# A fused attention and gated feed-forward kernel: attention steps gathered behind the first product, weights loaded in another order

## Chip, core and metric

The kernel runs on one core of a Trainium2 chip. A core has five engines that work at the same time, each through its own queue in order: TensorE (PE, matrix products), VectorE (DVE), ScalarE (ACT), GpSimd (POOL) and SyncE (SP, which here issues the transfers). The metric is the device time of one execution in microseconds (us).

## The reference

```python
B, H, S, D = 8, 8, 576, 64
scores = q @ k.T / sqrt(D)                       # per batch and head
gamma  = 1 - 2.0 ** (-5 - arange(H))
Dmat   = where(i >= j, gamma ** (i - j), 0)      # causal decay
x      = ((scores * Dmat) @ v)                   # to (B*S, H*D) = (4608, 512)
h      = x @ w_in                                # 512 -> 1024
u      = h * exp(h - max(h)) / sum(exp(h - max(h)))
ln     = (u - mean(u)) / sqrt(var(u) + 1e-6) * g_ln
out    = ln @ w_out                              # 1024 -> 512, float32
```

Attention has no softmax over positions: it is linear with a decay, so it can be done in chunks with a running state (the sum of k times v, decayed).

## The kernel before

The 4608 rows are worked in 36 chunks of 128 rows. The chunks of two batches alternate: for each pair of batches there are four chunks of each (c = 0 to 3), then one chunk made of the last 64 rows of both (c = 4). So a group of nine chunks repeats four times.

A chunk n goes through these steps, each a helper in the code:

- `ld` loads q, k and v (SP), `cast` scales q and v by powers of gamma and turns all three into 16 bit (three POOL instructions; for chunks 0 and 1 q on VectorE and k on ScalarE).
- `transpose_qk` turns q16 and k16 on TensorE into `tp`; `evict_qk` copies that to `qkT` (VectorE).
- `scores` makes `sc` (TensorE, half-size weights of 64 rows), `mask` multiplies it with a triangle `tris` into `ret` (VectorE, two instructions).
- `state` makes `kp` = k times v (TensorE, weights of 64 columns); `state_update` adds it on VectorE to the old state (`t`) and makes on POOL the decayed 16-bit copy `s16` and, for c < 3, the 32-bit `s32`.
- `values` makes `x` from `ret` and v (64 columns), and from the state (full weights, for c > 0); `evict_x` copies it to `xT` (ScalarE).
- `mm1`, the first product: `xT` by w_in into `h`, 8 matmuls. `row_max` (VectorE), `exps` (ScalarE, with the sum), `solu` (VectorE: u = h times e, its sum, and nmu, minus its mean).
- `spread` (ScalarE: sum of squares of u + nmu) and `root` (three tiny POOL instructions w1, w2, rs): the factor of the row.
- `transpose_u` (TensorE), `evict_u` (ScalarE), `mm2`, the second product by w_out, 8 matmuls, and `store` (ScalarE scales by rs, SP stores).

u itself is transposed, not u minus its mean. The mean is taken out through the weights: `mean_w_out` and `centre_w_out` subtract from w_out (times g_ln) the mean over its 1024 rows.

The order on every engine is the order in which the code is written (`tc.manual_schedule()`, line 469). A start written out by hand (lines 470 to 569) treats chunks 0 and 1 together, with both first products in one call, and the loop at line 571 runs i from 3 to 34. In row i TensorE does: transposes of q and k of i+1, first product i, scores i+1, second product i-2, state and values i+1, transposes of u i-1. POOL does: the casts of i+2, `root` of i-1, s16 and s32 of i+1. An end (lines 596 to 613) treats the last chunk in halves.

PSUM tiles other than `h` come from one pool of four (`ps`): a new tile waits until the one four before it has been read. Load tiles have six buffers.

The transfers stand on SP in this order: the small table, chunk 0, chunk 1, w_in in four pieces, w_out in four, chunks 2 to 5. The identity and the triangles are constants loaded on ScalarE's queue.

Of the kernel before, what the change touches and what calls it, by code (L numbers as in the profile page):

```python
# [12 lines left out]
P = 128  # L13
H = 8
D = 64
LAG = 2


def _np_tables():


    g = 1.0 - 2.0 ** (-5.0 - np.arange(H, dtype=np.float64))
    p = np.arange(P)
    gq = (g[None, :] ** p[:, None]) / 8.0
    gk = g[None, :] ** (-p[:, None])
    gqt = (g[None, :] ** (p % 64)[:, None]) / 8.0
    gkt = g[None, :] ** (-(p % 64)[:, None])


    gs = np.zeros((P, 4))  # L30
    gd = np.zeros((P, 4, 2))
    for e in range(2):
        for hp in range(4):
            gs[e * 64 : e * 64 + 64, hp] = g[2 * hp + e] ** 128.0
        gd[e * 64 : e * 64 + 64, :, e] = gs[e * 64 : e * 64 + 64]
    small = np.concatenate([gq, gk, gqt, gkt, gs, gd.reshape(P, 8)], axis=1).astype(np.float32)
    tri = (p[None, :] >= p[:, None]).astype(np.float32)
    trit = tri * ((p[None, :] // 64) == (p[:, None] // 64))
    tris = np.concatenate([tri, trit], axis=1).astype(np.float32)
    return small, tris, np.eye(P).astype(np.float16)  # L40
# [3 lines left out]
def kernel(  # L44
# [19 lines left out]
    small_np, tris_np, id_np = _np_tables()  # L64

    const = ctx.enter_context(tc.tile_pool(name="const", bufs=1))
    load = ctx.enter_context(tc.tile_pool(name="load", bufs=6))
    half = ctx.enter_context(tc.tile_pool(name="half", bufs=4))
# [3 lines left out]
    utp = ctx.enter_context(tc.tile_pool(name="utp", bufs=LAG + 1))  # L72
# [13 lines left out]

# [4 lines left out]

# [10 lines left out]
    w_in16 = const.tile([P, 4, DFF], F16, name="w_in16")  # L102
    w_out16 = const.tile([P, NF, DM], F16, name="w_out16")
    gq, gk = small[:, 0:8], small[:, 8:16]
# [4 lines left out]
    T = {}  # L109

# [12 lines left out]
    def cast(n, first=False):  # L123
        qf, kf, vf = T.pop(("ld", n))
        tail = chunks[n][1] == 4
        a, b = (gqt, gkt) if tail else (gq, gk)
        q16 = half.tile([P, H, D], F16, name="q16")
        k16 = half.tile([P, H, D], F16, name="k16")
        v16 = half.tile([P, H, D], F16, name="v16")
        eq = nc.vector if first else nc.gpsimd  # L130
        eq.tensor_tensor(  # L131
            out=q16, in0=qf, in1=a.unsqueeze(2).to_broadcast([P, H, D]), op=ALU.mult
        )
        if first:
            nc.scalar.copy(out=k16, in_=kf)
        else:
            nc.gpsimd.tensor_copy(out=k16, in_=kf)  # L137
# [3 lines left out]
        T["h", n] = q16, k16, v16  # L141

# [42 lines left out]
    def state(n):  # L185

        (b,), c = chunks[n][0], chunks[n][1]
        _, k16, v16 = T["h", n]
        kp = ps.tile([P, 4, D], FP, tag="ps", name="kp")
        for hp in range(4):  # L190
            for e in range(2):
                nc.tensor.matmul(  # L192
                    out=kp[64 * e : 64 * e + 64, hp], lhsT=k16[:, 2 * hp + e],
                    rhs=v16[:, 2 * hp + e], start=True, stop=True,
                )
        T["kp", n] = kp

    def state_update(n):
# [5 lines left out]
        else:  # L204
            nc.vector.tensor_tensor(out=t, in0=kp, in1=T["s32", b], op=ALU.add)  # L205

        s16 = stp.tile([P, 4, 2, D], F16, tag=f"s16_{b % 2}", name="s16")
# [11 lines left out]
    def values(n):  # L219
        bs, c = chunks[n]  # L220
        ret = T.pop(("ret", n))
        _, _, v16 = T.pop(("h", n))
        qkT = T.pop(("qkT", n))
        x = ps.tile([P, 4, P], FP, tag="ps", name="x")
        s16 = [T.pop(("s16", b, c)) for b in bs] if c > 0 else []
        w = P // len(bs)

        for hp in range(4):
            for e in range(2):
                nc.tensor.matmul(  # L230
                    out=x[64 * e : 64 * e + 64, hp], lhsT=v16[:, 2 * hp + e],
                    rhs=ret[e][:, hp], start=hp == 0, stop=not s16, skip_group_check=True,
                )
        for hp in range(4):
            for i, s in enumerate(s16):
                nc.tensor.matmul(  # L236
                    out=x[:, hp, i * w : (i + 1) * w], lhsT=s[:, hp].rearrange("p e d -> p (e d)"),
                    rhs=qkT[:, 0, hp, i * w : (i + 1) * w],
                    start=False, stop=i == len(s16) - 1, skip_group_check=True,
                )  # L240
        T["x", n] = x

# [6 lines left out]
    def mm1(*ns):  # L249

        xTs = [T.pop(("xT", n)) for n in ns]
        hs = [ps_h.tile([P, DFF], FP, tag="h", name="h") for n in ns]
        order = [(i, dc) for i in range(2) for dc in range(4)]
        if len(ns) > 1:
            order.sort(key=lambda o: o[1])
        for dc in range(4) if len(ns) > 1 else (None,):
            for xT, h in zip(xTs, hs):
                for i, d in order:
                    if dc in (None, d):
                        nc.tensor.matmul(  # L260
                            out=h[:, i * 512 : (i + 1) * 512], lhsT=xT[:, d],
                            rhs=w_in16[:, d, i * 512 : (i + 1) * 512],
                            start=d == 0, stop=d == 3,
                        )
        for n, h in zip(ns, hs):
            T["hps", n] = h
# [33 lines left out]
    def solu_halves(n):  # L300
        T["u", n] = []
        for h, (e, s) in zip(T.pop(("hps", n)), T["e", n]):
# [5 lines left out]
            T["u", n].append((u, su))  # L308

# [8 lines left out]

    def spread_halves(n):
        (u0, su0), (u1, su1) = T["u", n]  # L320
        (_, s0), (_, s1) = T["e", n]
        s, su, nmu = (tiny.tile([P, 1], FP, name=x) for x in ("s", "su", "nmu"))
        nc.vector.tensor_tensor(out=su, in0=su0, in1=su1, op=ALU.add)
        nc.vector.tensor_scalar(
            out=nmu, in0=su, scalar1=-1.0 / DFF, scalar2=None, op0=ALU.mult, op1=ALU.bypass
        )
        nc.gpsimd.tensor_tensor(out=s, in0=s0, in1=s1, op=ALU.add)
        sss = []
        for u in (u0, u1):
            sq = moe.tile([P, 512], F16, tag="sqh", name="sqh")  # L330
            ss = tiny.tile([P, 1], FP, tag="ssh", name="ssh")
            nc.scalar.activation(out=sq, in_=u, func=ACT.Square, bias=nmu, accum_out=ss)
            sss.append(ss)
        ss = tiny.tile([P, 1], FP, name="ss")
        nc.gpsimd.tensor_tensor(out=ss, in0=sss[0], in1=sss[1], op=ALU.add)
        root(n, s, ss)

    def row_max(n):
        nm = tiny.tile([P, 1], FP, name="nm")
        nc.vector.tensor_reduce(out=nm, in_=T["hps", n], axis=AX.X, op=ALU.max, negate=True)  # L340
        T["nm", n] = nm

    def exps(n):
        e = moe.tile([P, DFF], FP, name="e")
        s = tiny.tile([P, 1], FP, name="s")
        nc.scalar.activation(  # L346
            out=e, in_=T["hps", n], func=ACT.Exp, bias=T.pop(("nm", n)), accum_out=s
        )
        T["e", n] = e, s

    def solu(n):
        e, s = T["e", n]
        u = moe.tile([P, DFF], F16, name="u")
        su = tiny.tile([P, 1], FP, name="su")
        nmu = tiny.tile([P, 1], FP, name="nmu")
        nc.vector.scalar_tensor_tensor(  # L356
            out=u, in0=T.pop(("hps", n)), scalar=1.0, in1=e, op0=ALU.mult, op1=ALU.mult,
            accum_out=su,
        )
        nc.vector.tensor_scalar(  # L360
            out=nmu, in0=su, scalar1=-1.0 / DFF, scalar2=None, op0=ALU.mult, op1=ALU.bypass
        )
        T["u", n] = u, nmu

    def spread(n):

        u, nmu = T["u", n]
        _, s = T.pop(("e", n))
        sq = moe.tile([P, DFF], F16, name="sq")
        ss = tiny.tile([P, 1], FP, name="ss")  # L370
        nc.scalar.activation(out=sq, in_=u, func=ACT.Square, bias=nmu, accum_out=ss)  # L371
        root(n, s, ss)

    def root(n, s, ss):
        w1 = tiny.tile([P, 1], FP, name="w1")
        w2 = tiny.tile([P, 1], FP, name="w2")
        rs = tiny.tile([P, 1], FP, name="rs")
        nc.gpsimd.tensor_scalar(
            out=w1, in0=s, scalar1=s, scalar2=1e-6 * DFF, op0=ALU.mult, op1=ALU.mult
        )  # L380
        nc.gpsimd.tensor_tensor(out=w2, in0=w1, in1=ss, op=ALU.add)  # L381
        nc.gpsimd.tensor_tensor(out=rs, in0=w2, in1=mhalf, op=ALU.pow)  # L382
        T["rs", n] = rs

    def transpose_u(n):
        u, _ = T["u", n]
        lp = ps.tile([P, NF, P], F16, tag="ps", name="lp")
        for c in range(NF):
            nc.tensor.transpose(out=lp[:, c], in_=u[:, c * P : (c + 1) * P], identity=ident)  # L389
        T["lp", n] = lp  # L390

    def evict_u(n, copy=None):
        uT = utp.tile([P, NF, P], F16, name="uT")
        (copy or nc.scalar.copy)(out=uT, in_=T.pop(("lp", n)))  # L394
        T["uT", n] = uT

    def mm2(n, parts=1):

        uT = T.pop(("uT", n))
        T["o", n] = []  # L400
# [243 lines left out]
```

## Time and profile before

| | us |
|---|---|
| time, median of 3 runs | 236.75 (235.94 to 238.74) |
| span of the profiled execution, first to last instruction | 233.8 |
| first product of chunks 0 and 1 starts | 15.06 |
| first product of chunks 2, 3, 4, 5, 6, 7 starts | 32.18, 37.91, 43.50, 49.10, 55.00, 60.66 |
| first product of chunk 35 starts | 216.45 |
| first instruction on q(0), k(0), v(0) | 5.36, 6.81, 8.13 |
| ScalarE's casts of w_in's four pieces start | 12.86, 14.10, 15.64, 16.67 |
| cast of v(3) starts, after a wait for its transfer | 30.20 |

In the profile, "busy" is the time in which an engine works on an instruction. Matmuls are pipelined: a group starts when its first matmul does, and the pitch of the starts tells its cost (0.216 us for 512 columns, 0.056 for 128, at full clock). PE's clock is either full or half. Lines such as L208 are lines of the kernel below the heading above; x8 means eight instructions put together.

### The profile page before, as it was taken

The page shows a single profiled execution, that of the slowest core. Times are in us where ns is not written, and L with a number is a line of the kernel's source. Part 1 is how long each engine was busy: PE and PEld are TensorE (multiplying, and loading weights), DVE is VectorE, ACT ScalarE, POOL GpSimd, SP SyncE. Part 2 cuts the span into 40 slices and gives each one's busy share as a digit, 9 for nine tenths or more (in the row PEclk, how much of TensorE's full clock was granted, in tenths as well). Part 3 has the DMA queues.
Part 4 walks back from the last instruction along what each step waited for, and adds up shares of the span by engine and source line. Part 5 has one row for each costly group of instructions (what it writes and reads, how often), then busy time and mean ns, then how long its engine had stood idle before and what let it go on. Part 6 is the DMA issues. An engine that isn't in the chain of part 4 may idle for free.

```text
span 233.8 us, 5779 instructions
## 1 busy us (share of the span) xinstructions
PE 209.8 (90%) x2128; PEld 114.8 (49%) x2128; DVE 177.1 (76%) x304; ACT 169.4 (72%) x267; POOL 177.6 (76%) x282
## 2 busy tenths in 40 slices
PE   0584789999999999999999999999999999999770
PEld 0331454555555555555555555555555555555340
DVE  1536699888888888888888888888788888887610
ACT  2255395787877888888888887778788778888761
POOL 0287679999768998998959999998679999983020
PEclk9999799999999999999999999999999999999996
DMA  7999999999979885978888897888799773111113
GB/s 128 248 400 332 206 222 219 206 230 235 257 179 226 178 179 140 232 188 194 196 196 190 174 204 183 205 200 185 189 192 195 159 190 92 48 45 49 46 45 90
DMA packets 121084, 42.51 MB, mean 182 GB/s; under 512 B 114656, under 2 KB 115040, under 8 KB 121056
## 3 DMA queue, kind: packets, MB, share of 16 engines
q1 hardware_dynamic: 119728, 41.98, 78.0%
q10 hardware_dynamic: 1328, 0.17, 0.6%
q8 instruction: 16, 0.26, 0.5%
q14 instruction: 12, 0.10, 0.2%
HBM read 32.70 MB, written 9.44 MB: 180 GB/s over the span
## 4 chain that ended last, share of the span: by engine, by line
PE 77%; POOL 7%; DVE 4%; ACT 3%; issue 2%; DMA 2%; SPq 2%; POOLq 0%; ACTq 0%
PE o L405 25%; PE h L260 25%; PE tp L149 6%; PE lp L389 6%; PE sc L168 5%; PE x L230 3%; PE x L236 3%; PE kp L192 3%; DMA kf<-in_k_dram 2%; SPq L118 2%; POOL q L131 2%; POOL s L208 1%; PE mean L453 1%; DVE ret L181 1%; POOL v L138 1%
## 5 line engine op out<-in xcount | busy, mean ns | idle before, releaser
L405 PE MATMUL o<-w_out,uT 128*128 128x512 f16 (+1 forms) x296 | 68.4, 375 | 1.6 <-ACT uT L394 1.2
L260 PE MATMUL h<-w_in,xT 128*128 128x512 f16 x280 | 67.7, 386 | 0.5 <-ACT xT L246 0.2
L371 ACT ACTIVATE sq<-u,nmu 128x1024 f16<-128x1024 f16 x35 | 40.2, 1149 | 21.5 <-DVE nmu L360 21.5
L356 DVE SCALAR_TENSOR_TENSOR u<-h,e 128x1024 f16<-128x1024 f32 x35 | 42.8, 1224 | 6.6 <-ACT e L346 6.0
L181 DVE TENSOR_TENSOR ret<-sc,tris 128x512 f16<-128x512 f32 x72 | 46.0, 681 | 1.6 <-PE sc L168 1.6
L340 DVE TENSOR_REDUCE nm<-h 128x1 f32<-128x1024 f32 x35 | 42.4, 1214 | 4.9 <-PE h L260 4.9
L138 POOL TENSOR_TENSOR v<-vf,small 128x512 f16<-128x512 f32 x36 | 37.5, 1042 | 10.9 <-DMA vf<-in_v_dram 10.9
L405 PEld LDWEIGHTS <-uT 128*128 128x128 f16 x296 | 26.0, 98 | 30.8 <-ACT uT L394 1.9
L346 ACT ACTIVATE e<-h,nm 128x1024 f32<-128x1024 f32 x35 | 39.2, 1121 | 2.2 <-DVE nm L340 2.2
L157 DVE COPY qkT<-tp 128x1024 f16<-128x1024 f16 x34 | 23.5, 691 | 22.7 <-PE tp L149 22.7
L208 POOL TENSOR_TENSOR s<-t,small 128x512 f16<-128x512 f32 x32 | 33.3, 1042 | 7.3 <-DVE t L205 5.1
L260 PEld LDWEIGHTS <-xT 128*128 128x128 f16 x280 | 25.1, 99 | 27.8 <-ACT xT L246 1.6
L131 POOL TENSOR_TENSOR q<-qf,small 128x512 f16<-128x512 f32 x34 | 35.4, 1042 | 1.7 <-DMA qf<-in_q_dram 1.6
L417 ACT ACTIVATE o_sb<-o,rs 128x512 f32<-128x512 f32 (+1 forms) x37 | 24.9, 675 | 15.3 <-PE o L405 5.7
L394 ACT COPY uT<-lp 128x1024 f16<-128x1024 f16 x35 | 35.5, 1014 | 0.4 <-PE lp L389 0.4
L389 PE MATMUL lp<-ident,u 128*128 128x128 f16 x280 | 21.4, 219 | 3.7 <-DVE u L356 3.6
L246 ACT CAST xT<-x 128x512 f16<-128x512 f32 x36 | 21.0, 584 | 3.5 <-PE x L230 1.7
L381 POOL TENSOR_TENSOR w<-w,ss 128x1 f32<-128x1 f32 x36 | 6.8, 190 | 21.4 <-ACT sq L371 19.5
L382 POOL TENSOR_TENSOR rs<-w,mhalf 128x1 f32<-128x1 f32 x36 | 19.8, 549 | 2.8
L137 POOL CAST k<-kf 128x512 f16<-128x512 f32 x34 | 20.7, 610 | 1.2 <-DMA kf<-in_k_dram 1.2
L149 PE MATMUL tp<-ident,q 128*128 128x128 f16 x144 | 14.6, 226 | 6.3 <-DVE q L131 6.3
L389 PEld LDWEIGHTS <-u 128*128 128x128 f16 x280 | 16.6, 98 | 5.3 <-DVE u L356 4.7
(55 smaller groups left out, 215.6 us busy)
## 6 DMA issues: line engine op xcount, KB each, us to landing
qf<-in_q_dram SPq DMA_DIRECT2D x32, 256.0 KB, 4.0
kf<-in_k_dram SPq DMA_DIRECT2D x32, 256.0 KB, 4.7
vf<-in_v_dram SPq DMA_DIRECT2D x32, 256.0 KB, 4.9
out_dram<-o_sb SPq DMA_DIRECT2D x32, 256.0 KB, 2.6
w_in<-in_moe_w_in_dram SPq DMA_DIRECT2D x4, 512.0 KB, 5.7
w_out<-in_moe_w_out_dram SPq DMA_DIRECT2D x4, 512.0 KB, 9.1
qf<-in_q_dram SPq DMA_DIRECT2D x8, 128.0 KB, 3.7
kf<-in_k_dram SPq DMA_DIRECT2D x8, 128.0 KB, 3.5
```

The lines of the kernel that those rows point to most:

```text
L131: eq.tensor_tensor(out=q16, in0=qf, in1=a.unsqueeze(2).to_broadcast([P, H, D]), op=ALU.mult)
L138: nc.gpsimd.tensor_tensor(out=v16, in0=vf, in1=b.unsqueeze(2).to_broadcast([P, H, D]), op=ALU.mult)
L181: nc.vector.tensor_tensor(out=r, in0=sc[e], in1=m, op=ALU.mult)
L208: nc.gpsimd.tensor_tensor(out=s16, in0=t.unsqueeze(2).to_broadcast([P, 4, 2, D]), in1=gd.unsqueeze(3).to_broadcast([P, 4, 2, D]), op=ALU.mult,
L260: nc.tensor.matmul(out=h[:, i * 512 : (i + 1) * 512], lhsT=xT[:, d], rhs=w_in16[:, d, i * 512 : (i + 1) * 512], start=d == 0, stop=d == 3,)
L340: nc.vector.tensor_reduce(out=nm, in_=T["hps", n], axis=AX.X, op=ALU.max, negate=True)
L346: nc.scalar.activation(out=e, in_=T["hps", n], func=ACT.Exp, bias=T.pop(("nm", n)), accum_out=s)
L356: nc.vector.scalar_tensor_tensor(out=u, in0=T.pop(("hps", n)), scalar=1.0, in1=e, op0=ALU.mult, op1=ALU.mult, accum_out=su,)
L371: nc.scalar.activation(out=sq, in_=u, func=ACT.Square, bias=nmu, accum_out=ss)
L389: nc.tensor.transpose(out=lp[:, c], in_=u[:, c * P : (c + 1) * P], identity=ident)
L394: (copy or nc.scalar.copy)(out=uT, in_=T.pop(("lp", n)))
L405: nc.tensor.matmul(out=o, lhsT=uT[:, c], rhs=w_out16[:, c, i * w : (i + 1) * w], start=c == 0, stop=c == NF - 1,)
```

## The change

- **Order in a row.** `state` and `values` become one helper, `attend`: state products first, then kp, then the values. `state_update` is split into `state_sum` (VectorE) and `state_next` (POOL). In row i TensorE now does: first product i, `attend` i+1, scores i+2, transposes of u i-1, second product i-2, transposes of q and k i+3. So scores and casts run one chunk further ahead.
- **Casts.** Two pools (`qh` 3, `kvh` 5) take the place of `half` (4); load tiles have seven buffers, `utp` four. In the start `cast` puts k16 on ScalarE.
- **root.** w1 becomes `eps_term` (POOL), w2 moves to VectorE, rs stays on POOL.
- **Transfers.** The small table goes on ScalarE's queue; SP loads chunk 0, then w_in, then chunks 1 and 2, then w_out, then 3 to 5. Identity and triangles are made on POOL by `memset` and `affine_select`. w_in's second halves are cast on VectorE instead of POOL.
- **Centring.** For chunks 0 to 4 (`RAW = 5`) `solu` makes a further VectorE tile `uc` = u + nmu, which is transposed in place of u, and the second product takes uncentred weights `w_raw16`. The centred `w_out16` is made piece by piece in the rows and used from chunk 5 on.
- **Start and end.** Chunk 0 goes alone to the first product; rows 3 and 4 have an order of their own; the loop runs i from 5 to 34. In the end the second products of the last two chunks are cut in halves, and the last store uses two queues.

```diff
-    def cast(n, first=False):
...
+    def cast(n, ek=None):
+        cast_qk(n, None, ek)
+        cast_v(n)
...
+    def attend(n):
...
+        for hp in range(4):
+            for i, s in enumerate(s16):
+                nc.tensor.matmul(
+                    out=x[:, hp, i * w : (i + 1) * w], lhsT=s[:, hp].rearrange("p e d -> p (e d)"),
+                    rhs=qkT[:, 0, hp, i * w : (i + 1) * w],
+                    start=first, stop=False, skip_group_check=True,
+                )
...
+    def solu(n, centred=False):
...
+        if centred:
+            uc = moe.tile([P, DFF], F16, name="uc")
+            nc.vector.tensor_scalar(
+                out=uc, in0=u, scalar1=nmu, scalar2=None, op0=ALU.add, op1=ALU.bypass
+            )
+            T["ut", n] = uc
...
+    def root(n):
+        w2 = tiny.tile([P, 1], FP, name="w2")
+        rs = tiny.tile([P, 1], FP, name="rs")
+        nc.vector.tensor_tensor(out=w2, in0=T.pop(("w1", n)), in1=T.pop(("ss", n)), op=ALU.add)
+        nc.gpsimd.tensor_tensor(out=rs, in0=w2, in1=mhalf, op=ALU.pow)
...
         for a in range(4):
             load_w_in(a)
+        ld(1)
+        ld(2)
         for i in range(4):
             load_w_out(i)
...
+        for i in (3, 4):
+            mm1(i)
+            if i > 3:
+                evict_qk(i + 1)
+            scores(i + 1)
+            row_max(i)
+            mask(i + 1)
+            exps(i)
+            mm2(i - 1, raw=True)
+            attend(i + 1)
+            evict_x(i + 1)
+            state_sum(i + 1)
+            root(i - 1)
+            solu(i, i < RAW)
+            store(i - 1)
+            state_next(i + 1)
+            eps_term(i)
+            cast(i + 2, nc.scalar.copy)
+            transpose_u(i)
+            transpose_qk(i + 2)
+            evict_u(i)
+            spread(i)
+            centre_w_out(2 * i - 4, 2 * i - 3)
+            ld(i + 5)
...
-        for i in range(3, NCH - 1):
-            if on(i + 5):
-                ld(i + 5)
-            transpose_qk(i + 1)
-            evict_qk(i + 1)
...
+        for i in range(5, NCH - 1):
             if on(i + 5):
                 ld(i + 5)
+            mm1(i)
+            if i > 5:
+                solu(i - 1)
+            if on(i + 2):
+                evict_qk(i + 2)
+            attend(i + 1)
+            if i > 5:
+                spread(i - 2) if i > 6 else None
+            evict_x(i + 1)
+            if has_state(i + 1):
+                state_sum(i + 1)
+            if i > 5:
+                eps_term(i - 1)
+            if has_state(i + 1):
+                state_next(i + 1)
+            if on(i + 2):
+                scores(i + 2)
+            row_max(i)
+            if i > 6:
+                root(i - 2)
+            if on(i + 2):
+                mask(i + 2)
+            if i > 5:
+                transpose_u(i - 1)
+            exps(i)
+            if i > 5:
+                evict_u(i - 1)
+            if i > 6:
+                mm2(i - 2)
+                store(i - 2)
...
+            if on(i + 3):
+                cast(i + 3)
+                transpose_qk(i + 3)
```

## The prediction

> **What bounds the kernel now.** I read the page first (busy shares, 40 slices, chain of waits), then one chunk of the steady stage in the timeline, the clock in the windows, and the first 50 us. From the page:
>
> ```profile
> PE 209.8 (90%) x2128; PEld 114.8 (49%) x2128; DVE 177.1 (76%) x304; ACT 169.4 (72%) x267; POOL 177.6 (76%) x282
> ...
> PE   0584789999999999999999999999999999999770
> ...
> PE 77%; POOL 7%; DVE 4%; ACT 3%; issue 2%; DMA 2%; SPq 2%; POOLq 0%; ACTq 0%
> ```
>
> TensorE is full from slice 6 to 36, and the chain that ends last runs on it. One chunk of that stage (start, length, engine, line):
>
> ```profile
> 92.98 0.41 DVE L205 TENSOR_TENSOR t<-kp,s 128x256 f32<-128x256 f32 x1
> ...
> 93.47 1.04 POOL L208 TENSOR_TENSOR s<-t,small 128x512 f16<-128x512 f32 x1 [0.28 <-DVE t L205]
> ...
> 93.60 0.39 PE L149 MATMUL tp<-ident,k 128*128 128x128 f16 x4
> ...
> 93.83 1.90 PE L260 MATMUL h<-w_in,xT 128*128 128x512 f16 x8
> ...
> 94.47 0.61 POOL L216 TENSOR_TENSOR s<-t,small 128x256 f32<-128x256 f32 x1
> ...
> 95.04 1.04 POOL L131 TENSOR_TENSOR q<-qf,small 128x512 f16<-128x512 f32 x1
> ...
> 95.66 0.40 PE L168 MATMUL sc<-qkT 64*128 64x128 f16 x8
> ...
> 96.03 0.61 POOL L137 CAST k<-kf 128x512 f16<-128x512 f32 x1
> ...
> 97.82 0.32 PE L192 MATMUL kp<-v,k 128*64 128x64 f16 x8
> ...
> 98.24 0.55 POOL L382 TENSOR_TENSOR rs<-w,mhalf 128x1 f32<-128x1 f32 x1
> 98.29 0.23 PEld L236 LDWEIGHTS <-s 128*128 128x128 f16 x4
> 98.30 0.40 PE L236 MATMUL x<-qkT,s 128*128 128x128 f16 x4
> ```
>
> Two things are to be seen. TensorE starts a chunk every 5.60 us (93.83, then 99.42) without a gap. GpSimd (POOL) is nearly as full: from s at 93.47 to the next s at 99.07 it idles 0.28 us. But TensorE does not wait for it, because the transpose of k at 93.60 reads a k16 that POOL finished in the row of the chunk before.
>
> **The steady rows.** The change gives TensorE per row: first product i, attention (state, kp, values) i+1, scores i+2, transposes of u i-1, second product i-2, transposes of q and k i+3. POOL gets: s16 and s32 of i+1, rs of i-2, then the casts q, k, v of i+3. The built kernel's instruction order has it so in every row, and the transposes of q and k carry a wait for POOL. So a ring closes: kp(i+1) on TensorE, t on VectorE, then s16, s32, rs, q16, k16 on POOL, the transposes of that k16 on TensorE, and right behind them the first product i+1, which leads to kp(i+2). Before, the casts stood ahead of the same row's s16, and their transposes came a row later. "One more chunk of lead" is in what is computed; the cast and its transposes have lost a row.
>
> The ring by rows: first product 8 x 0.216 (pitch of its starts) = 1.73; four state products 0.23 (98.30 to the next group at 98.53); one change from full to half-size weights 0.10 (93.83 to 95.66 is 1.83, against 1.73); kp 0.32; to VectorE 0.04; then from t's start to k16's end in the rows above 96.64 - 92.98 = 3.66, plus rs, which now lies inside, 0.51; to TensorE 0.06; four transposes of k 0.23. Sum 6.88 us, against 5.60. Variants: the first chunk of a sequence lacks the state products, 6.65. The fourth has no s32 (-0.57), but then rs waits for w2 (now on VectorE behind the row maximum, 0.17), 6.47. The half chunk has neither kp nor s16: row maximum 1.21, w2 0.16, rs, q16, k16, transposes, about 5.7. Nine chunks: 2 x (6.65 + 6.88 + 6.88 + 6.47) + 5.7 = 59.5. Before, the starts of the first product 110.68 and 160.70 lie nine chunks apart: 50.0. The ring holds from the start of product 7 to that of 33: attention of chunks 8 to 33 is 5.7 + 2 x 59.5 + (2 x 6.65 + 4 x 6.88 + 6.47) = 172, where before took 205.32 - 60.66 = 144.7: **+27 us**. All other moved steps (mask, copies, exp, w2) lie inside this row's slack, since VectorE's busy share was 20.5 of 24 us at a pitch of 5.6.
>
> **What it saves on TensorE.** Changes between full weights and half-size ones (64 rows or 64 columns) cost about 0.10 us each; there were four in a row, now three (columns to rows counts: at 9.41, from scores to kp, the gap was 0.13 at half clock). With the ring at 6.88 over a TensorE content of 5.5 this lands in slack: zero. It would be 0.10 x 30 = 3 us if TensorE were still the bound.
>
> **The start.** The small table goes to another queue, so qf leaves SP 0.39 earlier, and w_in follows chunk 0 directly: v(0) was first read at 8.13, and the casts of w_in's pieces start 12.86 to 16.67, so pieces land 1.27 apart; the last now lands near 8.13 - 0.39 + 4 x 1.27 = 12.8 instead of 16.7. Masks on POOL: five instructions; the nearest rows are 0.10 (memset 128x1) to 1.04 (128x512), 0.5 to 5.2 us in sum; POOL idled to 8.13, and the identity, done after the first two, is needed near 5.0. Taken at nothing; the high end costs nothing either, as the identity comes first. First product 0 then starts near 12.0 and runs 8 x 0.43 (half clock, as at 15.06 before) to 15.6. From there one chunk goes through all engines in order: row maximum 1.2, exp 1.2, u 1.4, nmu 0.15, centring (bounds 0.15 to 1.2; the nearest row, TENSOR_SCALAR 128x512, is 0.48; taken 0.45) to 20.0; mask(1) queued behind it 1.2; attention(1) 0.8; on ScalarE uT(0) 1.0, xT(1) 0.6, k16(2) 0.6; its transposes; product 1 at 23.7. Product 1 at half clock 3.6, row maximum 1.2, mask(2) 1.2, attention 0.6, xT 0.6: product 2 at 30.9 (before 32.2). Product 2 to 33.0, row maximum, exp, u, centring and the scaling of w_out's seventh piece behind them on VectorE to 39.1; the mean and second product 0 to 41.9; w2(0) and rs(0) 39.1 to 39.7, and q16(3) behind rs on POOL to 40.7; transposes, qkT, scores (behind second product 1), w2(1), rs(1), q16(4), k16(4) on ScalarE behind uT(2) to 47.6; attention(3), xT(3): **product 3 at 47 to 49** (before 37.9). Rows 3 and 4 have a longer ring: product 1.95, row maximum 1.13, first half of mask 0.68 (it frees the PSUM tile that x needs), 0.15, state products and kp 0.64, t 0.41, w2 0.12, rs 0.56, s16 and s32 1.57, w1 0.22, q16 1.04, transposes 0.5 = 9.0 us. Then scores, mask and transposes of chunk 6 or 7 stand before product 5, some 2.3 more, and in rows 5 and 6 rs, queued behind mask, keeps the ring near 8 and 6. Product 7: 47 + 9.0 + 11.3 + 7.8 + 5.8 = 81, and half-clock stretches on top, taken as 3: **84** (before 60.7). The loads of chunks 6 and 7 stand on SP behind the stores of chunks 0 and 1 and leave near 46; their casts come after 65: nothing.
>
> The clock's rows:
>
> ```profile
> 18.00:21.40 3.40, 2.10 (x10) 0.78 (x8) 1.69 (x2) 1.16 (x2) 3.40 (x5) 1.00 1.06 378
> 21.40:24.80 3.40, 1.15 (x12) 0.80 (x13) 3.37 (x6) 2.51 (x5) 1.68 (x3) 1.00 1.34 229
> 24.80:28.20 3.40, 3.11 (x14) 1.47 (x12) 2.19 (x7) 0.25 (x1) 2.53 (x3) 0.50 1.30 215
> ```
>
> The first number after the comma is TensorE's busy time; the third from the end is the clock. 1.15 busy of 3.4 was followed by half clock, 2.10 was not. The start's gaps are of the first kind, two to four stretches at 1 to 2 us: 0 to 8, taken 3. In the ring TensorE is busy 5.5 of 6.88, far above 2.10 of 3.4: full clock.
>
> [...] VectorE's casts of w_in and centrings take the place of POOL's casts. In the trace POOL's k16 at 24.64 to 25.25 overlaps VectorE's scaling of w_out from 25.03, and both kept their length (0.61; two in 0.89): nothing is added. [...]
> POOL's first rows show no pause before a new kind of operation. [...]
>
> **The end.** Without casts, rows 33 and 34 are TensorE's again: 5.0 and 4.6 to the last first product (5.5 less 0.45 for the transposes of q and k, then less 0.4 for scores); before, 17.35 us followed its start to the span's end; the second products cut in halves and the last store on two queues save about 1 (the last ScalarE steps overlap more): 16.3.
>
> **Sum.** 84 + 172 + 5.0 + 4.6 + 16.3 = 282 us span against 233.8, and 236.75 - 233.8 = 2.95 beside the span: **285 us**.
>
> **Rivals.**
> 1. Faster: the ring does not bind, TensorE stays the bound. Price: product 2 is 1.3 earlier, 3 less by weight changes: about 232. It decides where t's start to k16's end fits into 2.8 us (5.5 less the 2.7 on TensorE and in hand-overs); the rows make it 4.17, and POOL's 1.04, 0.61 and 0.55 have the same length throughout. 3%.
> 2. The ring, but a start that loses no more than 5: product 7 at 66, total 267. For it: product 2 is early. Against it: rs, q16 and the transposes stand in one queue after another. 8%.
> 3. [...] 7%.
> 4. Parts cancel to within 1%: 2%.
> The forecast has 80%. The change does what it says as to order, so that it doesn't is no rival.
>
> **Range and chances.** From 271 (start 84 down to 76, ring less 0.1 a row) to 297 (half clock 8, port rule 4, first call 2). A measurement here tells about 1% (235.94 to 238.74 without a change). Faster 0.03, same 0.02, slower 0.95.
>
> **What would show it.** Right: first-product starts 6.5 to 6.9 apart in mid-kernel; the transposes of k waiting for POOL k in each row; TensorE near 80% there; POOL without idle between s16 and v; product 3 after 45. Wrong: a pitch below 5.7, or transposes that wait for nothing, ends the ring; product 7 before 68 ends the start.

## The result and the profile after

| | before | after | predicted |
|---|---|---|---|
| time, median of 4 runs each (us) | 237.51 (235.94 to 238.74) | 289.91 (288.98 to 292.66) | 285 (271 to 297) |
| span of the profiled execution | 233.8 | 287.3 | 282 |
| first products 0, 1, 2 start | 15.06 (0 and 1), 32.18 | 11.16, 23.18, 30.38 | 12.0, 23.7, 30.9 |
| first product 3 starts | 37.91 | 46.13 | 47 to 49 |
| first product 7 starts | 60.66 | 87.17 | 84 |
| first products 7 to 33 | 144.7 | 174.7 | 172 |
| first product 33 to the span's end | 28.5 | 25.4 | 25.9 |

The ratio is 1.224, with a 95% interval of 1.215 to 1.233. The 53.5 us between the spans are 26.5 up to product 7, 30.0 from there to product 33, and 3.1 won behind it. From the page of the changed kernel: the busy line, TensorE's 40 slices, and the chain of waits by engine and by line.

```profile
PE 224.8 (78%) x2136; PEld 122.9 (43%) x2136; DVE 188.1 (65%) x348; ACT 171.7 (60%) x276; POOL 170.3 (59%) x241
...
PE   1658677475779888888999888888898888889981
...
POOL 35%; PE 30%; issue 13%; DVE 8%; DMA 6%; ACT 5%; SPq 1%; POOLq 0%; DVEq 0%; ACTq 0%
PE h L267 18%; POOL q L126 11%; POOL s L242 10%; POOL k L130 6%; POOL rs L327 5%; PE tp L153 4%; DMA w_in<-in_moe_w_in_dram 3%; DMA kf<-in_k_dram 3%; DVE t L235 3%; PE kp L215 2%; POOL v L137 2%; POOL s L250 2%; PE o L349 2%; PE x L206 1%; ACT uT L339 1%
```

No engine is near full any more, TensorE included. POOL, with 59% the least busy of the four, carries 35% of the chain: what binds is an order. The timeline of one row in mid-kernel (start, length, engine, line, and in brackets the idle time ahead and who ended it) shows it; the first product before this one started at 128.43, 6.95 us earlier:

```profile
130.47 0.32 PE L215 MATMUL kp<-v,k 128*64 128x64 f16 x8
...
130.90 0.42 DVE L235 TENSOR_TENSOR t<-kp,s 128x256 f32<-128x256 f32 x1 [1.58 <-PE kp L215]
...
131.41 1.04 POOL L242 TENSOR_TENSOR s<-t,small 128x512 f16<-128x512 f32 x1 [2.02 <-DVE t L235]
...
132.40 0.61 POOL L250 TENSOR_TENSOR s<-t,small 128x256 f32<-128x256 f32 x1
...
132.97 0.55 POOL L327 TENSOR_TENSOR rs<-w,mhalf 128x1 f32<-128x1 f32 x1
133.49 1.04 POOL L126 TENSOR_TENSOR q<-qf,small 128x512 f16<-128x512 f32 x1
...
134.47 0.61 POOL L130 CAST k<-kf 128x512 f16<-128x512 f32 x1
...
135.14 0.40 PE L153 MATMUL tp<-ident,k 128*128 128x128 f16 x4 [0.16 <-POOL k L130]
...
135.38 0.81 PE L267 MATMUL h<-w_in,xT 128*128 128x512 f16 x3
```

From kp through t, s16, s32, rs, q16 and k16 to the transposes of k and the next first product, each step starts within 0.11 us of the end of the one before it, and POOL waits 2.02 us once a row for t. The waits view sums it (us, times, longest):

```profile
POOL s L242 <- DVE t L235: 48.2, 21, 5.5
PEld L153 <- POOL q L126: 41.1, 32, 2.6
...
DVE t L235 <- PE kp L215: 33.1, 22, 3.2
PE tp L153 <- POOL q L126: 26.7, 28, 2.1
```

Each of the three engines waits for the one before it in the ring. Before, the transposes did not wait for POOL in these rows.

### The profile page after: what moved, and what is told of

Its sections match the earlier page's. It is cut to its first block, busy times and chain, and to the rows that moved or that the text cites. A ratio compares the mean times of both kernels' runs of the same rounds, so it can differ in the third digit from the quotient of the medians.

```text
span 287.3 us, 5701 instructions
## 1 busy us (share of the span) xinstructions
PE 224.8 (78%) x2136; PEld 122.9 (43%) x2136; DVE 188.1 (65%) x348; ACT 171.7 (60%) x276; POOL 170.3 (59%) x241
## 4 chain that ended last, share of the span: by engine, by line
POOL 35%; PE 30%; issue 13%; DVE 8%; DMA 6%; ACT 5%; SPq 1%; POOLq 0%; DVEq 0%; ACTq 0%
PE h L267 18%; POOL q L126 11%; POOL s L242 10%; POOL k L130 6%; POOL rs L327 5%; PE tp L153 4%; DMA w_in<-in_moe_w_in_dram 3%; DMA kf<-in_k_dram 3%; DVE t L235 3%; PE kp L215 2%; POOL v L137 2%; POOL s L250 2%; PE o L349 2%; PE x L206 1%; ACT uT L339 1%
## 5 line engine op out<-in xcount | busy, mean ns | idle before, releaser
L267 PE MATMUL h<-w_in,xT 128*128 128x512 f16 x280 | 74.9, 416 | 2.9 <-ACT w_in L450 1.5
L242 POOL TENSOR_TENSOR s<-t,small 128x512 f16<-128x512 f32 x32 | 33.9, 1059 | 67.1 <-DVE t L235 48.2
L349 PE MATMUL o<-w_out,uT 128*128 128x512 f16 (+1 forms) x264 | 58.8, 366 | 1.2 <-DVE su L410 1.2
L281 ACT ACTIVATE e<-h,nm 128x1024 f32<-128x1024 f32 x35 | 39.0, 1115 | 32.8 <-DVE w L326 20.1
L267 PEld LDWEIGHTS <-xT 128*128 128x128 f16 x280 | 28.1, 106 | 34.0 <-issue 10.3
L153 PE MATMUL tp<-ident,q 128*128 128x128 f16 x144 | 15.3, 233 | 31.7 <-POOL q L126 26.7
L327 POOL TENSOR_TENSOR rs<-w,mhalf 128x1 f32<-128x1 f32 x36 | 19.8, 549 | 33.9 <-DVE w L326 33.3
L349 PEld LDWEIGHTS <-uT 128*128 128x128 f16 x304 | 28.1, 98 | 26.8 <-ACT uT L339 1.7
L126 POOL TENSOR_TENSOR q<-qf,small 128x512 f16<-128x512 f32 x35 | 37.3, 1066 | 0.0
L235 DVE TENSOR_TENSOR t<-kp,s 128x256 f32<-128x256 f32 x24 | 10.2, 424 | 33.1 <-PE kp L215 33.1
L153 PEld LDWEIGHTS <-q 128*128 128x128 f16 x144 | 8.8, 102 | 46.6 <-POOL q L126 41.1
L153 PE MATMUL tp<-ident,k 128*128 128x128 f16 x144 | 15.6, 236 | 6.8 <-POOL k L130 4.4
L334 PE MATMUL lp<-ident,u 128*128 128x128 f16 x240 | 18.3, 218 | 0.6
```

Of the source, the lines that this page charges most:

```text
L126: (eq or nc.gpsimd).tensor_tensor(out=q16, in0=qf, in1=(gqt if tail else gq).unsqueeze(2).to_broadcast([P, H, D]), op=ALU.mult,)
L153: nc.tensor.transpose(out=tp[:, i, hp], in_=s2[:, hp * P : (hp + 1) * P], identity=ident)
L242: nc.gpsimd.tensor_tensor(out=s16, in0=t.unsqueeze(2).to_broadcast([P, 4, 2, D]), in1=gd.unsqueeze(3).to_broadcast([P, 4, 2, D]), op=ALU.mult,
L267: nc.tensor.matmul(out=h[:, i * 512 : (i + 1) * 512], lhsT=xT[:, d], rhs=w_in16[:, d, i * 512 : (i + 1) * 512], start=d == 0, stop=d == 3,)
L281: nc.scalar.activation(out=e, in_=T["hps", n], func=ACT.Exp, bias=T.pop(("nm", n)), accum_out=s)
L349: nc.tensor.matmul(out=o, lhsT=uT[:, c], rhs=wt[:, c, i * w : (i + 1) * w], start=c == 0, stop=c == NF - 1,)
```

## The experiments

Theory: the ring through POOL makes the rows long, and a start that goes through the engines in order costs the rest. Rivals: TensorE's new order or its clock; POOL's sum of work; VectorE (w2); the order of the loads. "Pitch" is the distance of first products in mid-kernel, named by the chunk whose attention the row does (first to fourth, or half).

**1. Casts ahead.**

```diff
+            if on(i + 3):
+                cast(i + 3)
             mm1(i)
...
             if on(i + 3):
-                cast(i + 3)
                 transpose_qk(i + 3)
```

> The changed kernel, with one step put back in the rows from 5 on: the casts of chunk i+3 stand ahead of the first product i instead of behind s16, s32 and rs of the same row; their transposes stay where they are. Ring theory: the transposes of k no longer wait for POOL, TensorE's own content of about 5.5 us sets the row, and the starts of the first product come 5.3 to 5.6 apart in mid-kernel instead of 6.6 to 6.95. Products 7 to 33 then take about 144 instead of 174.7, rows 5 and 6 shrink a little too: span 253 to 259, time 256 to 262. Rival, TensorE's new order itself or its clock makes the row long: pitch stays at 6.6 to 6.95, time 288 to 291. Rival, VectorE (w2 behind the row maximum, on which rs waits 33 us in sum) makes it long: pitch falls only to about 6.2, time near 275.

Measured: 253.27 us (ratio to before 1.069, 1.059 to 1.078), pitch 5.27 for first chunks, 5.56 for second to fourth, 5.37 for half chunks. Timeline, one row, and the page's chain:

```profile
113.88 0.42 DVE L235 TENSOR_TENSOR t<-kp,s 128x256 f32<-128x256 f32 x1 [0.66 <-PE kp L215]
...
114.39 1.04 POOL L242 TENSOR_TENSOR s<-t,small 128x512 f16<-128x512 f32 x1 [0.64 <-DVE t L235]
...
116.75 0.39 PE L153 MATMUL tp<-ident,k 128*128 128x128 f16 x4
...
117.46 0.61 POOL L130 CAST k<-kf 128x512 f16<-128x512 f32 x1
```

```profile
PE 71%; DVE 8%; issue 7%; ACT 6%; POOL 5%; DMA 2%; POOLq 0%; SPq 0%; DVEq 0%; ACTq 0%
```

The transposes of k at 116.75 wait for nothing (their k16 was cast a row before; the one at 117.46 is the next chunk's), and the chain is TensorE's again. One step moved gives back about 37 us: products 7 to 33 take 143.5, where before took 144.7, and rows 5 and 6 take 9.8 instead of 16.4. The time is 2.7 below the expected range, which had these two rows shrink only a little. The rivals of TensorE's order and of VectorE fall: both are as they were.

**2. A dose: rs behind the casts.**

```diff
-                root(i - 2)
+                root(i - 2, True)
...
                 transpose_qk(i + 3)
+            if i > 6:
+                power(i - 2)
+                store(i - 2)
```

(`power` is the rs instruction of `root`.)

> The changed kernel, with rs (POOL) of the rows from 7 on and the store that needs it put behind the casts of the same row, so that q16 follows s32 directly. Ring theory: each round of the ring loses the 0.52 us of rs (where there is no s32, 0.6 to 0.7, since rs waited for w2 there): pitch 6.1 to 6.45 instead of 6.57 to 6.95, 26 rows by 0.5 to 0.6 are 13 to 16, time 274 to 277. Rival, TensorE or its clock makes the row long: no change, 288 to 291. Rival, POOL is simply full (a matter of its sum of work and not of the order): no change either, since POOL does the same work.

Measured: 278.31 us (1.177, 1.170 to 1.184). Pitch 6.14, 6.44, 5.86: products 7 to 33 take 160.3, 14.4 less, as the ring says; POOL does the same work, so its sum is not what binds. The half chunk's row does not get shorter (5.76): with rs out of its way TensorE no longer waits for POOL there, but 0.24 us for ScalarE's xT. The time is 1.3 above the expectation because product 7 came at 90.50, 3.3 later than in the changed kernel (see "What stays open").

**3 and 4. The old start, with the casts ahead and behind.** The kernel of experiment 1 with the start, loads and rows 3 to 5 of the kernel before, and the new rows from 6 on; row 5 takes up the extra chunk of lead (it also transposes, scores and masks chunk 7, and casts and transposes chunk 8). Then the same with the casts moved back:

```diff
-            if on(i + 3):
-                cast(i + 3)
             mm1(i)
...
             if on(i + 3):
+                cast(i + 3)
                 transpose_qk(i + 3)
```

> The start and rows 3 to 5 of the kernel before (its loads, masks and centred weights; w2 on POOL there), then the changed kernel's rows from 6 on with the casts ahead of the first product as in the first run of this call. If the start by itself is what is left of the loss: product 7 near 64 instead of 87, mid-kernel pitch 5.3 to 5.6, span 229 to 235, time 232 to 238, that is 22 to 26 below the first run. Rival, the start's loss comes from the rows' order as well (filling one more chunk of lead, wherever it is done): product 7 at 75 or later, time 245 or more. If three weight-mode changes in a row instead of four are worth 0.10 each, the pitch is 0.1 under that of the kernel before, and about 3 us of the 30 rows show.

> The run before this one with a single step moved: the casts of chunk i+3 again behind s16, s32 and rs, as in the changed kernel. Ring theory: pitch 6.57 to 6.95 (5.70 for the half chunk) from row 6 on, 27 rows by about 1.25 more, so 28 to 33 us above the run before it: 261 to 269. Rival, the ring only binds after the changed start (its half clock, its loads behind the stores): pitch stays near 5.5 and the time within 5 us of the run before it.

Measured: 234.09 us (0.991, 0.987 to 0.996) with the casts ahead: product 7 at 65.88 (in a profiled execution of 236.94), row 5, with the extra lead, 8.13. With the casts behind 265.93 us (1.125, 1.118 to 1.133), pitch 6.66, 6.95, 6.57 and 5.70, the same to 0.01 as in the changed kernel from row 8 on, but for one row. So the ring costs 31.8 us behind the old start too, and the changed start by itself 253.27 - 234.09, about 19 (22 to 26 were expected). The first of the two is the fastest order tried: faster than before by about 1%.

**5. No centring.**

```diff
-            solu(i, i < RAW)
+            solu(i)
...
-            centre_w_out(2 * i - 4, 2 * i - 3)
...
-        wt = w_raw16 if raw else w_out16
+        wt = w_raw16
```

(and the same in the start and ahead of row 5.) This kernel leaves out the subtraction of the mean, so it computes something else than the reference; it is there for its time alone.

> The changed kernel without the taking out of the mean (left out: the five uc of chunks 0 to 4 and the eight pieces of centre_w_out; every second product takes w_raw16). All waits between the other steps are as before. In the changed kernel POOL's operations beside these VectorE instructions were longer (q16 1.47 and s16 1.48 instead of 1.04, s32 0.80 and 1.06 instead of 0.61, w1 0.70 instead of 0.27). If VectorE's instructions on SBUF hold up POOL: these come back to 1.04, 0.61 and 0.27 in rows 3 and 4, each of rows 4 and 5 shortens by about 0.55 (uc) + 1.05 (POOL), the start gives back two uc as well, product 7 at 81 to 84 instead of 87.2, time 283 to 287. Rival, the POOL operations were long for another cause (their operands' transfers, their place in the start): same lengths, and only the uc are won, time 287 to 289.

Measured: 286.06 us (1.210, 1.201 to 1.218), product 7 at 82.83. POOL and VectorE in row 3 of the changed kernel, then POOL's same three instructions without centring:

```profile
52.56 0.55 DVE L310 TENSOR_SCALAR uc<-u,nmu 128x1024 f16<-128x1024 f16 x1
...
52.79 0.80 POOL L250 TENSOR_TENSOR s<-t,small 128x256 f32<-128x256 f32 x1
...
53.04 1.76 DVE L481 SCALAR_TENSOR_TENSOR w_out<-w_out,g,mean_sb 128x512 f16<-128x512 f32 x2
...
53.57 0.70 POOL L290 TENSOR_SCALAR w<-s 128x1 f32<-128x1 f32 x1
...
54.23 1.47 POOL L126 TENSOR_TENSOR q<-qf,small 128x512 f16<-128x512 f32 x1
```

```profile
52.11 0.61 POOL L250 TENSOR_TENSOR s<-t,small 128x256 f32<-128x256 f32 x1
52.70 0.26 POOL L290 TENSOR_SCALAR w<-s 128x1 f32<-128x1 f32 x1
52.92 1.04 POOL L126 TENSOR_TENSOR q<-qf,small 128x512 f16<-128x512 f32 x1
```

0.80, 0.70 and 1.47 become 0.61, 0.26 and 1.04: VectorE's instructions on SBUF held POOL up by 1.06 us in this row, on the way to product 4. Rows 3 and 4 fall from 10.42 and 14.21 to 9.03 and 11.82.

**6. Casts ahead in rows 3 and 4 too.** Experiment 1, and there

```diff
         for i in (3, 4):
+            cast(i + 2)
             mm1(i)
...
-            cast(i + 2, nc.scalar.copy)
```

(and the cast of chunk 7 ahead of `evict_qk(6)`).

> The first run's kernel (casts ahead of the first product from row 5 on), with the same done in rows 3 and 4 and for chunk 7, all on POOL. If the casts' place is the rest of the loss in these rows too, rows 3 and 4 fall from 24.6 us together to below 16 and the time from 253 to 245 or less. If instead these two rows are bound by one chunk going through the engines in order (product, row maximum, mask, attention, w2, rs), only q16 and v16 leave the chain: about 1 to 1.5 per row and 1 behind it, time 249 to 251.

Measured: 247.98 us (1.046, 1.039 to 1.054). Rows 3 and 4 take 18.7 instead of the 24.6 of experiment 1: between the two expectations. Part of these rows was the casts' place, more than q16 and v16 alone, though k16 also moved from ScalarE to POOL here; 7.5 us over the 11.2 of the kernel before remain, and no run takes them apart.

**7. Chunk 1 loaded ahead of w_in again.**

```diff
+        ld(1)
         for a in range(4):
             load_w_in(a)
-        ld(1)
```

> The changed kernel with the loads of chunk 1 ahead of w_in again, as in the kernel before; the rest unchanged. If w_in sooner is a gain by itself: product 0 about 3 us later (w_in's last piece lands behind 0.75 MB more), and the rest of the start after it, time 291 to 296. Rival, loading w_in ahead of chunk 1 delays chunk 1 and is what costs the start: product 1 earlier than 23.2, time 284 or less.

Measured: 292.60 us (1.240, 1.231 to 1.249), product 0 at 12.44, product 1 at 25.45, product 2 at 32.65. Products 1 and 2 are 2.3 later, where four kernels with the same code up to there (the changed one, experiments 1, 2 and 9) differ by 0.2 and 0.7: up to product 2, loading w_in sooner is a gain, though product 0 moved by 1.3 and not by 3. The 2.7 us between the times are no more than such starts differ by at product 3 (see "What stays open"), so they do not show the gain by themselves.

**8. Masks alone**, in the kernel before: identity and triangles by `memset` and `affine_select` on POOL, no loads for them.

> The kernel before, with only the identity and the triangles made on POOL by memset and affine_select instead of loaded. POOL is idle at that time: no change, 235.5 to 238.5. [...]

Measured: 236.23 us (0.996, 0.991 to 1.001), no change that can be told. The two `affine_select` took 0.29 and 0.41 us, the five instructions ran from 0.78 to 2.29, and the first transposes, for which q16 and not the identity came last, started at 5.58.

**9. More work for TensorE.** In rows 3 and 4 of the changed kernel:

```diff
+            fill(8)
             transpose_u(i)
+            fill(8)
             transpose_qk(i + 2)
```

(`fill(k)`: k products of `ident` by 512 columns of `w_in16` into a PSUM tile.)

> The changed kernel with work added: eight extra products of the identity by w_in (their result is read by nobody) ahead of the transposes of u, and eight ahead of the transposes of q and k, in rows 3 and 4, where TensorE waited 2.25 and 1.97 us in each row. Each eight take 1.7 us and fit into the wait. If half clock after those waits is part of the start's loss: the stretches at half clock at 55.8 and 66.1 go, first products 4 and 5 take 1.9 us instead of 3.23 and 2.95, product 7 comes at 83 to 85 instead of 87.2, time 285 to 288 although the kernel does more. Rival, the chain through the engines alone sets these rows: time 289 to 292.

Measured: 284.70 us (1.204, 1.197 to 1.211), 5.2 below the changed kernel. Windows of the two (after the comma TensorE's busy time; the clock is the third from the end), changed kernel first:

```profile
52.40:55.80 3.40, 0.66 (x9) 0.49 (x10) 2.37 (x4) 2.62 (x5) 3.40 (x5) 1.00 0.46 134
55.80:59.20 3.40, 3.40 (x15) 1.75 (x16) 0.69 (x1) 0.18 (x2) 0.90 (x1) 0.50 0.77 173
```

```profile
52.40:55.80 3.40, 2.98 (x34) 1.52 (x32) 3.11 (x8) 2.40 (x5) 2.09 (x3) 1.00 0.45 93
55.80:59.20 3.40, 3.16 (x27) 1.71 (x25) 1.79 (x3) 2.15 (x3) 3.34 (x4) 1.00 0.69 186
```

A stretch with 0.66 us of work was followed by one at half clock; with 2.98 it was not. Products 3 to 7 take 35.8 instead of 41.0, of which 3.9 are the first products 4, 5 and 6 themselves: 1.89 us each instead of 3.23, 2.95 and 3.41. The mean granted clock was 0.973 to 0.980 in the four executions, against 0.931 to 0.952.

**10 and 11. The old start with such a filler, and the masks.** Experiment 3 with `fill(16)` ahead of `transpose_u(0)`; then also the masks on chip and the small table on ScalarE's queue.

> The kernel with the old start and the new rows with casts ahead (234.1 us), with sixteen such extra products ahead of the transposes of u(0), where TensorE waits from about 21 to 25 us for the first u. If that wait is what puts the clock to half from 24.8 on: product 2 near 31 instead of 32 to 34, product 3 near 37, time 229 to 232. Rival, no effect, since the weights' centring on VectorE sets that stretch: 233.5 to 235.

> The run before this one with the masks made on chip and the small table on ScalarE's queue, as in the changed kernel. Masks alone moved all first products 0.9 us forward in one profile, with a time that could not be told from no change (ratio 0.991 to 1.001). Expected 0.3 to 1.3 us below the run before this one; if the half clock or the landing of w_in decides instead, no difference.

Measured: 233.85 us (0.991, 0.988 to 0.994) and 233.88 us (0.988, 0.983 to 0.993): neither differs from experiment 3. In the first the clock was full from 18.5 on, and product 2 came at 31.73; but so it was in experiment 4 without a filler, with product 2 at 31.71, while experiment 3, with the same start, had half clock from 23.1 to 29.9 and product 2 at 34.10. In the second, half clock came from 29.4 to 32.8 in spite of the filler: the eight transposes of u at 29.36 took 1.04 us where those at 23.94 took 0.62, and product 2 took 1.98 where the later ones took 1.89.

## Why the prediction was right, point by point

- **The ring.** Put at 6.88 for inner chunks, 6.65, 6.47 and 5.7 for the others; measured 6.95, 6.66, 6.57 and 5.70. Products 7 to 33 took 174.7 for 172; of the 2.7 over, 1.4 are row 7 alone, a half-chunk row that took 7.09 because the start's half clock reached into it (86.6 to 90.0). In the row shown, t's start to k16's end is 4.18 (put at 3.66 + 0.51 = 4.17), and the 0.07 is in the hand-over from kp to t: 0.43 from start to start, put at 0.32 + 0.04. Experiments 1, 2 and 4 take it away, shorten it and rebuild it. Rival 1, that it does not bind, is out; product 7 at 87 rules out rival 2 (66), and the time lies below the 297 at which the range ends, though half clock (5.2 and 1.4 us by experiment 9) and VectorE's instructions beside POOL's (1.06 us in row 3 by experiment 5) did add to it.
- **Weight-mode changes.** Put at 0.10 a row, lost in the ring's slack. With the ring open (experiment 1) nine chunks take 49.3 where before took 50.0: 0.08 a row on average, but 0.18 in rows of first chunks and 0.02 to 0.04 in those of second and third. One change less in every row, at one price, would save the same in each; so it is not shown that the gain comes from the weight changes.
- **The start up to product 3.** 46.13, put at 47 to 49. The steps named there are in the trace: rs(0) 37.40, q16(3) 37.93, rs(1) 40.94, q16(4) 41.71, k16(4) 43.62, but 1.7 (rs(0)) to 3.4 us (k16(4)) before the times put for their ends. As three kernels with the same code had product 3 at 48.6 to 49.7, that 46.13 is so near to the 47 of the sum is in part luck. No run took this chain apart; that it sets product 3 is read, not shown.
- **Rows 3 to 6.** Put at 9.0, 11.3, 7.8 and 5.8 (33.9) plus 3 for the clock; measured 10.42, 14.21, 8.77 and 7.64 (41.0). Two terms were mis-sized. **"Nothing is added"** for VectorE and POOL on SBUF: it was about 1.1 us in row 3, and without centring rows 3 and 4 measure 9.03 and 11.82. The overlap that the prediction had read was too short to tell: 0.22 us, where in the changed kernel the first 0.14 to 0.2 us of such an overlap do not show in the lengths (see the last section). In row 3 s32 took 0.80 beside `uc`, w1 0.70 and q16 1.47 beside the centring pieces, against 0.61, 0.26 and 1.04 without them in experiment 5: 0.19 to 0.44 us an instruction. In the start s32(0), which began 0.17 us into a cast of w_in, took 0.79 at 10.86. What this cost before product 3 no run shows. **"Half clock taken as 3"**: experiment 9 puts it at 5.2 in these rows and at 1.4 more in row 7 (5.71 instead of 7.09), and at full clock its rows 5 and 6 measure 7.79 and 5.80, what the sum had for them.
- **The first call.** No run shows the 2 us that the range has for it: the first `affine_select` took 0.29 us at 1.06, and experiment 8 shows no loss (0.996). Masks at nothing was right.
- **w_in sooner.** Product 0 at 11.16, put at 12.0: it starts on the pieces that are there and waits for the last one, cast at 13.53. A gain of 2.3 us at product 2 (experiment 7), in a start that loses 26.5 by product 7.
- **The end.** 25.4, put at 5.0 + 4.6 + 16.3 = 25.9.
- **The range.** Its lower end does not follow from its terms: 285 less 8 for the start and 0.1 for each of 26 rows is 274, not 271. Nothing hangs on it here. In its upper end the 4 us for a port rule are shown by no run; what the runs showed in their place is the 1.06 us of row 3, and 3.85 us less time (286.06 for 289.91) where the instructions that take out the mean are left out altogether.

What stays open: product 3 came anywhere from 46.13 to 49.68 in four kernels whose code is the same up to it (this one, experiments 1, 2 and 9; 46.13, 48.77, 49.68, 48.56), with the stretches at half clock in different places (none between 28.5 and 45 in this one, a mean clock of 0.57 in 31.6 to 35.0 and in 38.4 to 41.8 in experiment 1). Experiments 3 and 4 have the old start in common and product 3 at 40.99 and 37.44. So a difference of up to 3.5 us between two starts here proves nothing by itself.

## What to carry to other kernels

Before moving a step to another place in a row, follow each queue round from the step's output to the instruction behind it: here a ring over three engines set the row though each of them idled (TensorE was busy for 78% of the span, POOL for 59%), and the busy shares did not show it, while the chain (POOL 35%) and the waits by pairs did. The price of a ring could be added up here from the durations of the profile before, to about 1% a row; the price of the start, in which TensorE idles, only to several us, as the clock (5.2 us in rows 3 to 6) and the waits between VectorE and POOL (1.06 us in row 3) added to it. If such a ring shows, look for a step that needs nothing from the ring (here the casts) and move it ahead; that gave back 32 to 37 us here, with no engine made faster.

## What the runs showed of the hardware that was not expected

- **Extra work made the kernel faster**: 32 products more, 5.2 us less. The clock is 1.00 from 52.4 to 76.2, where the changed kernel has half clock in 55.8 to 59.2 and 66.1 to 72.9, and the first products 4 to 6 are 3.9 us shorter in sum, so most of the gain came through the clock.
- **The clock changed in steps of 3.4 us.** In the changed kernel, between 14.9 and 284.5, it was half in 18.3 to 28.5, 55.8 to 59.2, 66.1 to 72.9, 79.7 to 83.1 and 86.6 to 90.0: each length and distance is a multiple of 3.41 within 0.1. Not explained is that it stayed half for 10.2 us from 18.3, while TensorE was busy for 2.6 to 3.1 us of each 3.4. Nor does the busy time of a stretch by itself decide what follows: 1.46 us (35.4 to 38.8) was followed by the full clock, 1.89 us (83.1 to 86.6) by half.
- **POOL beside VectorE on SBUF**: 1.04 became 1.48, 0.61 became 0.80 to 1.06, 0.26 became 0.70. Where POOL started second beside `uc`, a centring piece or a cast of w_in, its instruction ended a fixed time after VectorE's: q16 and s16 0.90 us, s32 0.47, w1 0.13, each 0.14 less than its usual length (1.04, 0.61, 0.27). So what such an instruction took beyond its usual length was its overlap with VectorE's, less 0.14 us. For s32 in row 3 that instruction is `uc`, for w1 and q16 the centring pieces.
- **VectorE beside POOL was longer in the same way.** Two centring pieces took 1.76 to 2.19 beside POOL, but 1.41 at 71.24, where POOL was idle; before, with the mean read from PSUM, two took 1.41 too (27.10), beside a q16 that kept its 1.04. One that ran into s32 or w1 ended 0.54 to 0.55 us after it, 0.2 less than the usual 0.74.
